# Idle products at the start against a later copy in the w3 stage: a retention and feed-forward kernel on one core

## The chip, the cores and the metric

The kernel runs on one core of a Trainium2 chip. The metric is the device time in microseconds (us) of one execution; the median of three is 869.62 us (869.52 to 870.43). The profile shows one execution, with a span of 867.7 us from the first instruction to the last. Its engines are TensorE (PE, with PEld for its weight loads), VectorE (DVE), ScalarE (ACT), GpSimd (POOL) and SyncE (SP, which only issues transfers here).

## The reference

Retention (attention with a decay in place of a softmax), and behind it a multiplicative feed-forward network, all in float32 except for the weights, which arrive as 64-bit floats and are converted to float32 in the kernel:

```python
# q, k, v: (8, 8, 576, 64);  w1, w2: (512, 1024);  w3: (1024, 1024);  w_out: (1024, 512)
scores = matmul(q, k^T) / sqrt(64)
gamma  = 1 - 2 ** (-5 - arange(8))                    # one per head
ret    = scores * where(rel >= 0, gamma ** rel, 0)    # rel = row - column
x      = matmul(ret, v) -> (4608, 512)                # tokens x (heads * 64)
a, b   = x @ w1, x @ w2
out    = (a * b @ w3) @ w_out
```

The kernel multiplies w3 by w_out first (the product is called w3o) and applies it to the tokens as one matrix.

## The kernel before

Retention works on chunks of 64 or 128 rows of two batches at a time: `front` transposes k and q on TensorE (ScalarE copies them out), `score` makes the products of q and k (VectorE masks them), `state` carries k and v to the next chunk, and `pv` makes the tokens xT. `up` is one part of x @ w1 and x @ w2, in Strassen's form: seven products of sums of tiles, called S, T and the like. The sums T of the tokens are made by `strassen_tokens`, the first of them on VectorE.

The weights are converted in pieces of 128 x 512, by hand from the bits of the 64-bit floats. A piece takes five VectorE instructions and two of ScalarE (cut to its core):

```python
def begin_block():
    ...
    vec.tensor_scalar(out=e, in0=hi, ...)                 # exponent bits
    yield
    vec.tensor_scalar(out=m, in0=hi, ...)                 # mantissa, high part
    yield
    vec.scalar_tensor_tensor(m, in0=lo, ..., in1=m)       # and low part
    nc.scalar.activation(e, e, relu, bias=lim[:, 0:1], scale=-1.0)
    nc.scalar.activation(e, e, relu, bias=lim[:, 1:2], scale=-2.0 ** 23)
    yield

def end_block():
    vec.scalar_tensor_tensor(e, in0=hi, ..., in1=e)       # sign; waits for ScalarE
    yield
    ...
    vec.scalar_tensor_tensor(out, in0=m, ..., in1=e)      # the float32 piece
    if key[0] == "w3" and key[2] == DF // CV - 1:         # second half of a w3 tile
        yield
        t = pools["wst"].tile([P, KF, P], F32, tag="w3T", name="w3T", bufs=3)
        vec.transpose(t..., live["w3"]...)
        live["w3T", key[1]] = t
    ...
```

`convert(n)` lets this go on by n steps, so the conversion of the next piece is spread between other work. One piece is begun before the last one is ended. With a w3 tile of 128 rows ready and transposed, TensorE multiplies it by w_out, in one accumulator, and ScalarE copies it out:

```python
def w3_mm(ft):
    ps = acc.tile([P, DM], F32, tag="acc", name="ps")
    for g in range(KF):
        nc.tensor.matmul(ps, live["w3T", ft][:, g, :], live["wo"][:, g, :],
                         start=(g == 0), stop=(g == KF - 1))
    nc.scalar.copy(live["w3o"][:, ft, :], ps)
    multiplied[0] += 1
...
while multiplied[0] < KF:
    ...
    if ready or not todo:
        convert_up_to(done)
        w3_mm(ft)
    if not todo:
        convert(11)
```

`acc` has seven accumulator banks. Eleven steps of conversion are one tile of w3, which is two pieces and a transpose.

At the start the kernel also issues products of the identity by itself, whose result nobody reads:

```python
warm = acc.tile([P, P], F32, tag="acc", name="idle")
for _ in range(10):
    nc.tensor.matmul(warm, ident, ident, start=True, stop=True)

def keep_busy(n):
    t = acc.tile([P, P], F32, tag="acc", name="idle")
    for _ in range(n):
        nc.tensor.matmul(t, ident, ident, start=True, stop=True)
...
scale(0, "q")
front(0, "k")
keep_busy(4)
front(0, "q")
...
scale(1, "q")
front(1, "k")
keep_busy(6)
front(1, "q")
...
pv(1)
keep_busy(4)
load(3, "kqv")
...
up(0, 0, 0, conv=2, tail=False, busy=8)    # keep_busy(8) behind its first product
```

Of the kernel before, what the change touches and what calls it, by code (L numbers as in the profile page):

```python
# [8 lines left out]
F32 = mybir.dt.float32  # L9
# [31 lines left out]
def kernel(  # L41
# [13 lines left out]
    nc = tc.nc  # L55
# [6 lines left out]
    P = 128  # L62
# [37 lines left out]
    acc = ctx.enter_context(tc.tile_pool(name="acc", bufs=7, space=PSUM))  # L100
# [4 lines left out]
    live = {}  # L105
# [14 lines left out]
    ident = const.tile([P, P], F32, tag="ident", name="ident")  # L120
# [13 lines left out]
    nc.scalar.dma_start(dq, decay_q)  # L134
    nc.scalar.dma_start(gk[:short, 0, :], decay_k[:short, :])
    nc.scalar.dma_start(gk[:, 1:, :], decay_k[short:, :].rearrange("(c p) h -> p c h", p=P))
    warm = acc.tile([P, P], F32, tag="acc", name="idle")
    for _ in range(10):
        nc.tensor.matmul(warm, ident, ident, start=True, stop=True)
    gps = acc.tile([P, NC, H], F32, tag="acc", name="gps")  # L140
    for c in range(NC):
        nc.tensor.transpose(gps[:sizes[c], c, :], dq[:, starts[c]:starts[c] + sizes[c]], ident[:H, :H])
    for c in (0, slice(1, NC)):
        n = short if c == 0 else P
        nc.vector.tensor_copy(gq[:n, c, :], gps[:n, c, :])

    def keep_busy(n):

        t = acc.tile([P, P], F32, tag="acc", name="idle")
        for _ in range(n):  # L150
            nc.tensor.matmul(t, ident, ident, start=True, stop=True)

# [4 lines left out]
    def A(fp, nm):  # L159

        h, m = divmod(fp, 2)
        if nm in ("S1", "S2", "S4"):
            return wS[h][:, ("S1", "S2", "S4").index(nm), m]
        r, f = {"A11": (0, 0), "A12": (1, 0), "A21": (0, 1), "S3": (0, 1), "A22": (1, 1)}[nm]
        return wA[h][:, :, 2 * r:2 * r + 2, m * QC + f * P:m * QC + f * P + P]
# [48 lines left out]
    def scale(g, nm, scalar=False):  # L214
        c = g % NC
        sz = sizes[c]
        t, gam = live[nm, g], {"q": gq, "v": gk}[nm]
        t = t[:sz].rearrange("p (b h) d -> p b h d", b=2)
        if scalar:
            for h in range(H):  # L220
                nc.scalar.mul(t[:, :, h, :], t[:, :, h, :], gam[:sz, c, h:h + 1])
            return
        nc.gpsimd.tensor_tensor(  # L223
            out=t, in0=t, in1=gam[:sz, c].unsqueeze(1).unsqueeze(3).to_broadcast([sz, 2, H, D]), op=ALU.mult)

    def front(g, names="kq"):
        c = g % NC
        sz = sizes[c]
        for nm in names:
            src = live[nm, g]  # L230
            dst = pools["fr"].tile([P, 2, NP, P], F32, tag=nm + "T", name=nm + "T",
                                   bufs=1 if nm == "k" and g >= NC else 2)
            for b in range(2):
                tp = acc.tile([P, NP, P], F32, tag="acc", name="tp")
                for p in range(NP):
                    h = b * H + 2 * p
                    nc.tensor.transpose(tp[:, p, :sz],  # L237
                                        src[:sz, h:h + 2, :].rearrange("p a d -> p (a d)"),
                                        ident[:sz, :sz])
                nc.scalar.copy(dst[:, b, :, :sz], tp[:, :, :sz])  # L240
            live[nm + "T", g] = dst
# [197 lines left out]
    def go_on():  # L439
        while converting:  # L440
            r = next(converting[-1], "end")
            if r != "end":
                return r
            converting.pop()
        return "end"

    def convert(n):

        for _ in range(n):
            if go_on() is not None:  # L450
                return

    def convert_up_to(n):
        while converted[0] < n:
            assert go_on() is None


    def w3_mm(ft):
        ps = acc.tile([P, DM], F32, tag="acc", name="ps")
        for g in range(KF):  # L460
            nc.tensor.matmul(ps, live["w3T", ft][:, g, :], live["wo"][:, g, :],  # L461
                             start=(g == 0), stop=(g == KF - 1))
        nc.scalar.copy(live["w3o"][:, ft, :], ps)
        multiplied[0] += 1

    every = [(i, n) for i in range(NB2) for n in range(NB)]

    def has_x(i, n):
        return any(starts[c] + sizes[c] >= (n + 1) * TB and ("x", i * NC + c) in live for c in range(NC))

    def strassen_tokens(i, n, engine=nc.gpsimd):

        m = every.index((i, n))
        x = live["xT", m]
        B = [[x[:, 2 * r:2 * r + 2, b, :] for b in range(2)] for r in range(2)]
        T = [(t_first if m == 1 and j == 2 else ffn).tile(
            [P, 2, TB], F32, tag="T", name="T", bufs=1 if m == 1 and j == 2 else 5) for j in range(3)]

        def minus(out, in0, in1):
            engine.tensor_tensor(out=out, in0=in0, in1=in1, op=ALU.subtract)  # L480

        live["B", i, n] = {"B11": B[0][0], "B21": B[1][0], "B22": B[1][1], "T3": B[0][1],
                           "T1": T[0], "T2": T[1], "-T4": T[2]}
        minus(T[0], B[0][1], B[0][0])
        minus(T[1], B[1][1], T[0])
        minus(B[0][1], B[1][1], B[0][1])
        minus(T[2], B[1][0], T[1])

    def up(i, n, fp, conv=0, tail=True, busy=0):
        m = every.index((i, n))  # L490
        while ("S", fp) not in live:
            assert go_on() is None
        if ("B", i, n) not in live:
            strassen_tokens(i, n)
        if fp == 0:
            live["ab", i, n] = (pools["ab3"] if m == 2 else ffn).tile([P, 2 * KF, TB], F32, tag="ab", name="ab")
        ab = live["ab", i, n]

        def product(ps, a, b):
            a, b = A(fp, a), live["B", i, n][b]  # L500
            new = ps is None
            if new:
                ps = acc.tile([P, 2, TB], F32, tag="acc", name="up")
            for w in range(2):
                for r in range(2):
                    nc.tensor.matmul(ps[:, w, :], a[:, w, r, :], b[:, r, :], start=(new and w == r == 0),  # L506
                                     stop=(w == r == 1), skip_group_check=True)
            return ps

        def plus(ps, to, sb):  # L510
            nc.vector.tensor_add(c[:, to], ps, c[:, sb])  # L511
            convert(conv)
            if aside:
                aside.pop(0)()


        c = ffn.tile([P, 4, 2, TB], F32, tag="c", name="c", bufs=1)
        p1 = product(None, "A11", "B11")
        nc.scalar.copy(c[:, 0], p1)  # L519
        if busy:  # L520
            keep_busy(busy)
        plus(product(None, "S2", "T2"), 1, 0)
        plus(product(None, "S3", "T3"), 2, 1)
        p5 = product(None, "S1", "T1")
        plus(p5, 3, 2)
        plus(product(None, "A22", "-T4"), 2, 2)
        product(p1, "A12", "B21")
        nc.scalar.copy(c[:, 0], p1)  # L528
        product(p5, "S4", "B22")
        plus(p5, 1, 1)  # L530

        if fp == NQ - 1 and m + 1 < len(every) and has_x(*every[m + 1]) and ("B", *every[m + 1]) not in live:
            strassen_tokens(*every[m + 1])
        nc.vector.tensor_mul(ab[:, 4 * fp:4 * fp + 4, :], c[:, :, 0, :], c[:, :, 1, :])  # L534
        if tail:
            convert(conv)
# [130 lines left out]
    load(1, "v")  # L667
    load_block()
    scale(0, "q")
    front(0, "k")  # L670
    keep_busy(4)
    front(0, "q")
    convert(3)
    score(0)
    scale(0, "v")
# [6 lines left out]
    convert_up_to(2)  # L682
    load_block()
    scale(1, "q")
    front(1, "k")
    keep_busy(6)
    front(1, "q")
    convert(3)
    scale(1, "v")
    score(1)  # L690
# [4 lines left out]
    first_sums = strassen_weights(0)  # L695
    next(first_sums)
    pv(1)
    keep_busy(4)
    load(3, "kqv")
    load_block()  # L700
    strassen_tokens(0, 0, nc.vector)
# [1 line left out]
        pass  # L703
    scale(2, "q", True)
    aside.append(lambda: scale(2, "v", True))
    up(0, 0, 0, conv=2, tail=False, busy=8)
    front(2)
    convert(1)
    scale(3, "q")
# [12 lines left out]
    score(3)  # L722
    aside.extend([lambda: None] * 3 + [lambda: scale(4, "q", True)])
    up(0, 0, 1, conv=2)
    front(4)
    pv(3)
# [21 lines left out]
    todo = [(0, 1, 2), (0, 0, 3), (0, 1, 3)] + [(0, 2, fp) for fp in range(NQ - 1)]  # L748
    while multiplied[0] < KF:
        ft = multiplied[0]  # L750
        done = at["w3", ft, DF // CV - 1] + 1
        ready = converted[0] >= done
        if todo:
            first = converted[0] < 4 * NQ
            up(*todo.pop(0), conv=2 if first else 1)
            convert(0 if first else 3)
        if ready or not todo:
            convert_up_to(done)
            w3_mm(ft)
        if not todo:  # L760
            convert(11)
    w3_part.close()


# [15 lines left out]
    todo = [(down, (0, 0), (0, 1)), (down, (1, 0), (1, 1)), (down, (0, 2), (1, 2))]  # L780
# [38 lines left out]
    for g in range(NC, G):  # L819
        c = g % NC  # L820
        n = -(-len(todo) // (NC - c))
# [78 lines left out]
```

## Time and profile before

| | busy us | share of the span |
|---|---|---|
| TensorE, products | 849.2 | 98% |
| TensorE, weight loads (beside the products) | 774.4 | 89% |
| VectorE | 468.4 | 54% |
| ScalarE | 186.0 | 21% |
| GpSimd | 113.7 | 13% |

| tiles of the change | what the profile has |
|---|---|
| idle products | 64 records, from 1.4 to 32.6 us (each product is recorded twice) |
| product of w3 and w_out | 128 records of 128 x 512, from 158.4 to 216.8 us |
| ScalarE's copy of it | 8 instructions, median 586 ns, from 165.5 to 217.4 us |

The page lists the engines' busy time, the span in 40 slices with the granted clock of TensorE, the chain of work that ended last, and groups of instructions. In a group, a line such as "L463 ACT COPY w3o<-ps" names the line of the kernel, the engine, the operation, and the tile written and read. The idle time next to it is that of the engine just before the instruction, and an arrow names what ended it. The share of 98% is a mean over the whole kernel, so the two stages in question have to be looked at by windows: about 0 to 50 us for the idle products, and about 158 to 217 us for the product of w3 and w_out.

### The profile page before, as it was taken

How to read it: one execution, taken by the hardware profiler on the slowest of the kernel's cores; microseconds unless marked ns; L12 is line 12 of the kernel's file. 1: busy time of each engine (PE TensorE's matmuls, PEld its weight loads, DVE VectorE, ACT ScalarE, POOL GpSimd, SP SyncE). 2: the span in 40 equal slices, each digit the busy share in tenths (PEclk: the TensorE clock that was granted, in tenths of full speed). 3: DMA queues.
4: the chain of work that ended last, by engine and by line, in shares of the span. 5: the costliest groups of instructions: out<-in, count | busy, mean ns of one | idle time of the engine just before them, and what ended most of it. 6: DMA issues, size and time to landing. Idle time of an engine off the chain costs nothing.

```text
span 867.7 us, 15391 instructions
## 1 busy us (share of the span) xinstructions
PE 849.2 (98%) x6373; PEld 774.4 (89%) x6373; DVE 468.4 (54%) x789; ACT 186.0 (21%) x374; POOL 113.7 (13%) x91
## 2 busy tenths in 40 slices
PE   7999999999999999999999999999999999999998
PEld 6889999544888999999999999999999999999996
DVE  4889998986643334543544443534553435334343
ACT  3666333343122221101011101111101100001000
POOL 3000020001202223202123030230300101000000
PEclk9999999999999999999999999999999999999999
DMA  9993443444245534515242325061300000000001
GB/s 194 218 223 110 99 98 101 130 134 66 43 92 124 114 50 78 95 27 101 44 85 39 67 57 109 15 122 19 56 25 26 2 25 1 25 25 0 25 1 49
DMA packets 194629, 63.21 MB, mean 73 GB/s; under 512 B 176632, under 2 KB 184824, under 8 KB 194560
## 3 DMA queue, kind: packets, MB, share of 16 engines
q1 hardware_dynamic: 161920, 54.07, 29.8%
q10 hardware_dynamic: 32640, 8.16, 4.8%
q8 instruction: 50, 0.82, 0.4%
q14 instruction: 19, 0.16, 0.1%
HBM read 52.76 MB, written 9.44 MB: 72 GB/s over the span
## 4 chain that ended last, share of the span: by engine, by line
PE 84%; DVE 6%; issue 2%; ACT 1%; DMA 1%; SPq 0%; DVEq 0%; ACTq 0%
PE up L506 44%; PE po L614 24%; PE ps L461 4%; PE sc L252 4%; PE xps L309 3%; PE xps L302 2%; DVE c L511 2%; PE tp L237 1%; PE st L274 1%; DVE e L400 1%; DVE w L411 1%; DVE m L386 0%; DVE w3T L415 0%; DMA raw<-in_moe_w_out_dram 0%; ACT e L389 0%
## 5 line engine op out<-in xcount | busy, mean ns | idle before, releaser
L511 DVE TENSOR_TENSOR c<-up,c 128x384 f32<-128x384 f32 x240 | 133.2, 555 | 187.0 <-PE up L506 182.2
L506 PE MATMUL up<-xT,wA 128*128 128x192 f32 x1152 | 212.0, 327 | 0.0
L506 PEld LDWEIGHTS up<-xT,wA 128*128 128x128 f32 x1152 | 190.7, 190 | 2.5 <-issue 0.7
L506 PE MATMUL up<-T,wS 128*128 128x192 f32 x768 | 140.6, 326 | 0.0
L506 PEld LDWEIGHTS up<-T,wS 128*128 128x128 f32 x768 | 127.4, 190 | 0.2 <-issue 0.2
L614 PE MATMUL po<-w3o,ab 128*128 128x256 f32 x456 | 104.4, 380 | 2.2 <-DVE ab L580 1.7
L614 PEld LDWEIGHTS po<-w3o,ab 128*128 128x128 f32 x456 | 85.8, 190 | 14.5 <-DVE ab L580 2.1
L618 DVE TENSOR_TENSOR ot<-po,ot 128x256 f32<-128x256 f32 x90 | 38.2, 424 | 73.2 <-PE po L614 70.3
L528 ACT COPY c<-up 128x384 f32<-128x384 f32 x48 | 22.9, 478 | 225.8 <-PE up L506 221.6
L506 PE MATMUL up<-xT,wS 128*128 128x192 f32 x384 | 70.7, 327 | 0.6 <-DVE c L511 0.5
L255 DVE TENSOR_TENSOR pm<-sc,mask 128x512 f32<-128x512 f32 (+1 forms) x80 | 45.4, 629 | 46.4 <-PE sc L252 46.4
L506 PE MATMUL up<-T,wA 128*128 128x192 f32 x384 | 70.2, 326 | 0.0
L614 PE MATMUL po<-wB,forms 128*128 128x256 f32 x288 | 65.1, 379 | 0.0
L506 PEld LDWEIGHTS up<-xT,wS 128*128 128x128 f32 x384 | 63.5, 190 | 1.7 <-DVE c L511 1.7
L506 PEld LDWEIGHTS up<-T,wA 128*128 128x128 f32 x384 | 63.7, 190 | 0.0
L614 PEld LDWEIGHTS po<-wB,forms 128*128 128x128 f32 x288 | 54.7, 190 | 7.4
L223 POOL TENSOR_TENSOR ld_v<-ld_v,gk 128x1024 f32<-128x1024 f32 (+1 forms) x17 | 33.7, 1983 | 210.2 <-DMA ld_v<-in_v_dram 196.2
L461 PE MATMUL ps<-wo,w3T 128*128 128x512 f32 x128 | 56.1, 596 | 2.9 <-DVE w3T L415 2.9
L461 PEld LDWEIGHTS ps<-wo,w3T 128*128 128x128 f32 x128 | 23.8, 190 | 34.5 <-issue 30.6
L480 POOL TENSOR_TENSOR T<-xT,T 128x384 f32<-128x384 f32 x20 | 20.9, 1044 | 216.5 <-PE up L506 214.8
L534 DVE TENSOR_TENSOR ab<-c 128x768 f32<-128x768 f32 x48 | 46.4, 966 | 3.8
L519 ACT COPY c<-up 128x384 f32<-128x384 f32 x48 | 22.9, 477 | 116.3 <-PE up L506 67.4
(77 smaller groups left out, 814.2 us busy)
## 6 DMA issues: line engine op xcount, KB each, us to landing
raw<-in_moe_w_dram SPq DMA_DIRECT2D x64, 128.0 KB, 3.0
out_dram<-ot SPq DMA_DIRECT2D x24, 256.0 KB, 2.1
bl_q<-in_q_dram SPq DMA_DIRECT2D x136, 32.0 KB, 2.1
bl_k<-in_k_dram SPq DMA_DIRECT2D x136, 32.0 KB, 2.1
raw<-in_moe_w_dram SPq DMA_DIRECT2D x8, 512.0 KB, 7.7
raw<-in_moe_w_dram SPq DMA_DIRECT2D x16, 256.0 KB, 6.3
ld_k<-in_k_dram SPq DMA_DIRECT2D x8, 512.0 KB, 7.1
ld_q<-in_q_dram SPq DMA_DIRECT2D x8, 512.0 KB, 9.6
```

The lines of the kernel that those rows point to most:

```text
L223: nc.gpsimd.tensor_tensor(out=t, in0=t, in1=gam[:sz, c].unsqueeze(1).unsqueeze(3).to_broadcast([sz, 2, H, D]), op=ALU.mult)
L252: nc.tensor.matmul(sc[j][:sz, p, :sz], kT[hs, b, p, :sz], qT[hs, b, p, :sz], start=True, stop=True)
L255: nc.vector.tensor_mul(pm[:sz, b, j, :, :sz], sc[j][:sz, :, :sz], mask[:sz, :sz].unsqueeze(1).to_broadcast([sz, NP, sz]))
L309: nc.tensor.matmul(banks[r][heads[half], b, n, :sz], vs[:sz, b * H + 2 * p + j, :], pm[:sz, b, j, p, :sz], start=(c == 0 and m == 0), stop ...
L461: nc.tensor.matmul(ps, live["w3T", ft][:, g, :], live["wo"][:, g, :], start=(g == 0), stop=(g == KF - 1))
L506: nc.tensor.matmul(ps[:, w, :], a[:, w, r, :], b[:, r, :], start=(new and w == r == 0), stop=(w == r == 1), skip_group_check=True)
L511: nc.vector.tensor_add(c[:, to], ps, c[:, sb])
L519: nc.scalar.copy(c[:, 0], p1)
L528: nc.scalar.copy(c[:, 0], p1)
L534: nc.vector.tensor_mul(ab[:, 4 * fp:4 * fp + 4, :], c[:, :, 0, :], c[:, :, 1, :])
L614: nc.tensor.matmul(ps[nm], a[A][:, f, :], live["W"][B][:, f, :], start=(f == 0 and not on), stop=(f == NP - 1), skip_group_check=True)
L618: nc.vector.tensor_add(ot[:, to[0], to[1]], ps[nm], ot[:, sb[0], sb[1]])
```

## The change

All the idle products are taken out. They are there to fill TensorE's waits at the start. In their place, `w3_mm` no longer copies its result itself but returns the copy, and the loop issues it behind the conversion steps of the next tile. ScalarE works its instructions off in the order of issue, so the next tile's exponents no longer stand behind a copy that waits for the product.

```diff
-    warm = acc.tile([P, P], F32, tag="acc", name="idle")
-    for _ in range(10):
-        nc.tensor.matmul(warm, ident, ident, start=True, stop=True)
...
-    def keep_busy(n):
-
-        t = acc.tile([P, P], F32, tag="acc", name="idle")
-        for _ in range(n):
-            nc.tensor.matmul(t, ident, ident, start=True, stop=True)
...
-        nc.scalar.copy(live["w3o"][:, ft, :], ps)
         multiplied[0] += 1
+        return lambda: nc.scalar.copy(live["w3o"][:, ft, :], ps)
...
-    def up(i, n, fp, conv=0, tail=True, busy=0):
+    def up(i, n, fp, conv=0, tail=True):
...
-        if busy:
-            keep_busy(busy)
...
-    front(0, "k")
-    keep_busy(4)
-    front(0, "q")
+    front(0)
...
-    front(1, "k")
-    keep_busy(6)
-    front(1, "q")
+    front(1)
...
     pv(1)
-    keep_busy(4)
...
-    up(0, 0, 0, conv=2, tail=False, busy=8)
+    up(0, 0, 0, conv=2, tail=False)
...
-            w3_mm(ft)
-        if not todo:
-            convert(11)
+            evict = w3_mm(ft)
+
+            if not todo:
+                convert(11)
+            evict()
```

Every other instruction is the same, on each engine in the same order: TensorE has 32 products fewer, and on ScalarE six of the eight copies stand two pieces (four instructions) later.

## The prediction

> **What bounds the kernel now.** I read the engine totals and the slices of the page first, then the tensor engine's own order of time in the two stages that the change touches, and only then the waits there.
>
> ```profile
> PE 849.2 (98%) x6373; PEld 774.4 (89%) x6373; DVE 468.4 (54%) x789; ACT 186.0 (21%) x374; POOL 113.7 (13%) x91
> PEclk9999999999999999999999999999999999999999
> ```
>
> TensorE (PE) is busy 849.2 of 867.7 us, so at most 18.5 us of the span are PE standing still. A change off PE's path is worth nothing, and one that opens or closes PE gaps is worth those gaps. Two stages have them: the first 50 us, and the stage 158 to 217 us in which w3 is converted, transposed and multiplied by w_out.
>
> The second view is PE's order of time in the w3 stage. Columns: start, busy time, engine, line, operation, output<-inputs, shape, count, and in brackets the idle time before it and what ended it.
>
> ```profile
> 166.76 13.97 PE L461 MATMUL ps<-wo,w3T 128*128 128x512 f32 x32 [1.31 <-DVE w3T L415]
> 181.58 14.10 PE L461 MATMUL ps<-wo,w3T 128*128 128x512 f32 x32 [0.84 <-DVE w3T L415]
> 196.42 20.96 PE L461 MATMUL ps<-wo,w3T 128*128 128x512 f32 x48 [0.75 <-DVE w3T L415]
> ```
>
> Sixteen records are one tile, so a tile costs PE about 20.96 / 3 = 6.99 us or, in the run of two, 13.97 / 2 = 6.99; starts lie some 6.9 us apart. Three gaps, 2.90 us in all, wait for VectorE's transposed tile. Why VectorE is late shows in the same window over all engines:
>
> ```profile
> 173.91 0.59 ACT L463 COPY w3o<-ps 128x512 f32<-128x512 f32 x1 [5.09 <-PE ps L461]
> 174.39 0.72 ACT L389 ACTIVATE e<-e,lim 128x512 int32<-128x512 int32 x1
> 175.15 0.72 ACT L390 ACTIVATE e<-e,lim 128x512 int32<-128x512 int32 x1
> ...
> 175.90 0.69 DVE L400 SCALAR_TENSOR_TENSOR e<-raw,e 128x512 int32<-128x512 int32 x1 [1.08 <-ACT e L390]
> ```
>
> ScalarE sits 5.09 us before its copy of the product, because the product is not finished; the exponent work behind it in the queue was ready (its VectorE input began at 169.35 and takes 0.43). VectorE then waits 1.08 us for that exponent, and its transpose comes late for PE's tile at 181.58. The view of waits from 160 to 212 us has three such VectorE waits, 2.9 us in all.
>
> The third view is the clock in the first stage, in windows of 3.4 us (window, length, PE busy, granted clock, share of the transfers):
>
> ```profile
> 11.60:15.00 3.40, 2.12 (x65) 1.00 1.34 211
> 15.00:18.40 3.40, 3.40 (x17) 0.50 1.19 280
> 18.40:21.80 3.40, 1.70 (x13) 1.00 0.96 188
> 21.80:25.20 3.40, 2.59 (x50) 1.00 1.12 216
> ```
>
> The clock was halved for one such window after a sparse one, and restored after a full one. The idle products show the same from the inside:
>
> ```profile
> L151 PE MATMUL idle<-ident x44: 273/275/417, 7.5 to 32.6; 128*128 128x128 f32 x44
> L139 PE MATMUL idle<-ident x20: 274/421/582, 1.4 to 5.2; 128*128 128x128 f32 x20
> ```
>
> Median 421 ns in the first burst against 275 ns later: the kernel also starts slow, until about 4.8 us. The clock column reads 1.00 there, so it doesn't show the state before the first change.
>
> The fourth view is where the first stage has slack:
>
> ```profile
> 28.79 0.69 DVE L400 SCALAR_TENSOR_TENSOR e<-raw,e 128x512 int32<-128x512 int32 x1 [0.48 <-ACT e L390]
> ...
> 32.23 0.56 DVE L480 TENSOR_TENSOR T<-xT,T 128x384 f32<-128x384 f32 x1
> ...
> 44.59 1.06 PE L237 MATMUL tp<-ident,ld_k 128*128 128x128 f32 x8 [1.63 <-DMA ld_k<-in_k_dram]
> ...
> 48.91 1.09 PE L237 MATMUL tp<-ident,ld_q 128*128 128x128 f32 x8 [0.18 <-POOL ld_q L223]
> ```
>
> VectorE is nearly full from 23.1 to 35 us and makes the sums T that the first feed-forward product needs at 32.94. But PE still waits 1.63 us at 44.59 for a load of k, then 0.18 us for the scaled q. The chain of waits, followed back from 225 us, ends at 48.86, just before that last transpose: what comes before is set by transfers (busy share about 1 through the first 60 us), not by PE.
>
> **What the Trainium skill says.** "TensorE: Matmul & The Clock Gate", Part 1 ("What's actually happening"), says that TensorE starts at half clock, that a busy free-running window of about 3.4 us releases it, and that an idle one brings the half back. The trace agrees in the length: 15.00 to 18.40 us at 0.50. It doesn't agree that only idle windows throttle: 11.60 to 15.00 was 2.12 us busy, with products on 64 of the rows and columns. Part 4 of that page ("PE-mode transpose") says that transposes don't count as busy in the same way; no run here separates that. The table at its head says that ScalarE's queue is strictly in order while TensorE's isn't; the 5.09 us wait in front of ready exponents agrees.
>
> **The change, part by part.** (1) It removes 32 idle products (10 + 4 + 6 + 4 + 8), 64 records. By themselves they save nothing: the first ten lie before the decay load lands (6.39), the four before the scaled q (next product at 9.06, idle ones done at 8.64), the six at 16.66 to 19.0 before the q at 20.57, the four at 28.68 to 29.84 beside the copy of xT that ends at 29.71, and the eight end at 32.93 with T done at 32.79: at most 0.15 us.
>
> (2) What they bought is the clock. Without them PE starts its real work at 6.39 at half speed; the transposes at 14.96 measured what that means, 4 in 1.05 us against about 0.55 for 4 warm. Up to 20.57 nothing is lost, since that start is set by a load of q that landed at 18.6. From there, if still cold: the two score groups take 4.1 us in place of 2.06, the transposes and copies before them about 0.5 more, so VectorE's masked scores end at about 28.1 in place of 25.57, some 2.5 us late. Everything VectorE does up to T moves with that. If the clock is back by 21.8, the lateness is about 0.5 us; by 25.2, about 1.9; by 28.6 or 32, 2.5 to 3; if only at 35 to 39, then state, xps and the first product run cold too (1.15 + 1.10 + 1.97 + 1.47 = 5.7 us of warm work doubled) and the lateness is 4.4 to 6.3. The slack at 44.59 and 48.91 takes 1.63 + 0.18 = 1.8 us off each. The transfers themselves don't move: the load queue from 20 to 42 us is held by its own backlog (one issue of q lasts from 34.33 to 41.47), and the buffers that they reuse come free earlier. Loss: 0; 0.1; about 1; 2.6 to 4.5. With weights 0.4, 0.2, 0.15 and 0.25 the mean is about 1.1 us.
>
> (3) It moves ScalarE's copy behind the four exponent instructions of the next tile's two pieces. VectorE's order is the same. Its unhindered tile is seen at 165.37 to 172.21, transpose to transpose: 6.84 us. After the third transpose (done at 173.46) the fourth is then done at about 180.3, and PE finishes its third tile at about 180.6: the wait of 0.84 goes. So does the 0.75, by the same step. The 1.31 before 166.76 stays, because there VectorE was busy with the sums of the last feed-forward piece and ScalarE's exponents were not in the way. Gain: 0.84 + 0.75 = 1.6 us. The copy comes later, but its readers start at 220.56, after the last copy, which has no exponents left before it. After 217 us PE is busy to the end nearly without gaps, and the loads of the next batch are released by VectorE's last conversion, which moves forward too: the 1.6 us carry.
>
> Sum: 869.6 + 1.1 - 1.6 = 869.1 us. I put it at 869.3, a little higher, because the losses have the longer tail.
>
> **The rivals.** First, that the clock comes back as early as before: the work from 6.4 to 20 us, stretched by the half clock, is denser, which releases it. For it: 18.40 to 21.80 stayed at full clock with 1.70 us busy. Then the loss is nothing and the time 868.0. Second, that quarter-size products and transposes don't release it and it stays half until full-size products have filled a window, at 39 or even 42 us. For it: 11.60 to 15.00 throttled at 62% busy. Then the loss is 4.5 to 6 and the time 872.5 to 874. Third, that PE takes VectorE's place at once in the w3 stage, so that fewer than 1.6 us come out: 6.84 against about 6.9 leaves only a few hundredths a tile; a late piece of w3 would bring the wait back, and the gain would be 0.8. Fourth, that the copies, now late, hold accumulator banks: seven are there and this stage uses two or three, so I give it nothing.
>
> **Range and chances.** 867.8 is the gain with no loss and a little over; 873.5 the second rival without its far end. 2% are 17.4 us; PE's whole work between 6 and 39 us is smaller than twice that, and most of it is covered. Faster by over 2%: 0.005; within: 0.985; slower by over 2%: 0.01.
>
> **What would show it.** In the w3 stage of the changed kernel PE should show one gap of about 1.3 us and then a run of 112 records without a break; VectorE's wait for ScalarE's exponent should be gone. If the gaps are still there, step 3 is wrong. The transposes before 10 us should take twice 0.71; the clock column tells when full speed comes, and PE's start of the first product on T (32.94 before) less 1.8 tells the loss. If the transposes of ld_k at 44.59 begin later because their load came later, the claim that the transfers don't move is wrong. If the time is over 874, the half clock reaches farther than any case above.

## The result and the profile after

| | median us | range | ratio to before (95%) |
|---|---|---|---|
| before, beside it | 869.82 | 868.95 to 870.43 | |
| changed | 865.72 | 865.15 to 867.54 | 0.9958 (0.9945 to 0.9971) |
| changed, again, on another chip | 866.37 | 865.69 to 867.35 | 0.9963 (0.9950 to 0.9976) |

By the ratios the change takes off 3.7 and 3.2 us (by the medians 4.1 and 2.9), where 0.3 were predicted, 869.3 against 869.6: the time lies below the predicted range. TensorE (PE) is still busy for 98% of the span. The page of the changed kernel:

```profile
PE 844.1 (98%) x6309; PEld 770.1 (89%) x6309; DVE 465.6 (54%) x789; ACT 186.5 (22%) x374; POOL 113.7 (13%) x91
```

Busy PE fell by 5.1 us. The idle products alone were 10.7 us of it (4.08 + 1.16 + 2.35 + 1.16 + 1.95), and some 6 us came back because the products up to 25 us take longer without them; a total like this doesn't tell where the time went. PE's order of time does. First the w3 stage of the changed kernel (start, busy time, engine, line, operation, tiles, shape, count, idle before):

```profile
157.62 7.03 PE L452 MATMUL ps<-wo,w3T 128*128 128x512 f32 x16
165.96 48.38 PE L452 MATMUL ps<-wo,w3T 128*128 128x512 f32 x112 [1.31 <-DVE w3T L406]
```

One gap of 1.31 us, then 112 records without a break, as the prediction asked for; the next product starts at 214.18. ScalarE and VectorE in the same stage, with the copy where it stands now:

```profile
166.91 0.72 ACT L381 ACTIVATE e<-e,lim 128x512 int32<-128x512 int32 x1
167.10 0.68 DVE L391 SCALAR_TENSOR_TENSOR e<-raw,e 128x512 int32<-128x512 int32 x1
167.54 0.57 ACT L455 COPY w3o<-ps 128x512 f32<-128x512 f32 x1
```

The copy has no idle time in front of it, and the VectorE instruction that sets the sign starts without a wait. Before, the copy sat 5.09 us and VectorE 1.08. Six of the eight copies run so; the last two, with no exponents behind them, still wait for their product (4.94 and 6.28 us).

Then the first 50 us of the changed kernel, PE again:

```profile
21.65 3.79 PE L243 MATMUL sc<-qT,kT 64*128 64x128 f32 x32
...
34.11 1.54 PE L497 MATMUL up<-T,wS 128*128 128x192 f32 x8 [2.09 <-DVE T L471]
...
43.97 1.04 PE L228 MATMUL tp<-ident,ld_k 128*128 128x128 f32 x8
...
48.28 1.09 PE L228 MATMUL tp<-ident,ld_q 128*128 128x128 f32 x8 [0.20 <-POOL ld_q L214]
```

The scores run 3.79 us in place of 2.06. That is taken here as the half clock; the clock column reads 1.00 throughout, as it does at the start of the kernel before. The first product on T is 1.2 us late (34.11 against 32.94). At 43.97 nothing of that is left: the transposes of k no longer wait for the load, and those of q wait 0.20 us for GpSimd as before (0.18).

The rest of the gain lies behind the w3 stage, where the products of the tokens with w3o ("po") begin. VectorE's four sums of w3o and GpSimd's (POOL) scaling of the next batch's second chunk, in the kernel before:

```profile
221.22 2.32 POOL L223 TENSOR_TENSOR ld_q<-ld_q,gq 128x1024 f32<-128x1024 f32 x1 [3.68 <-DMA ld_q<-in_q_dram]
223.50 2.88 POOL L223 TENSOR_TENSOR ld_v<-ld_v,gk 128x1024 f32<-128x1024 f32 x1
```

```profile
222.16 2.46 DVE L551 TENSOR_TENSOR wB<-w3o 128x1024 f32<-128x1024 f32 x1
...
225.01 2.45 DVE L551 TENSOR_TENSOR wB<-w3o,wB 128x1024 f32<-128x1024 f32 x1
...
227.85 1.21 DVE L551 TENSOR_TENSOR wB<-w3o,wB 128x1024 f32<-128x1024 f32 x1
...
230.18 3.72 PE L614 MATMUL po<-w3o,ab 128*128 128x256 f32 x16 [1.74 <-DVE ab L580]
```

and after the change, when the scaling of q runs from 214.79 and only that of v meets a sum:

```profile
216.90 1.90 POOL L214 TENSOR_TENSOR ld_v<-ld_v,gk 128x1024 f32<-128x1024 f32 x1 [0.21 <-DMA ld_v<-in_v_dram]
```

```profile
217.52 2.36 DVE L540 TENSOR_TENSOR w3o<-w3o 128x1024 f32<-128x1024 f32 x1
...
220.28 1.21 DVE L540 TENSOR_TENSOR wB<-w3o 128x1024 f32<-128x1024 f32 x1
...
225.81 3.72 PE L603 MATMUL po<-w3o,ab 128*128 128x256 f32 x16 [0.50 <-DVE ab L569]
```

Before, two sums took twice their 1.21 us while GpSimd was scaling; after, one did. PE's wait for the VectorE work behind the sums fell from 1.74 to 0.50 us. The scaling falls earlier against the sums because the loads of the next batch start earlier. The first of them follows a VectorE instruction of the conversion, the one that sets the sign. Before:

```profile
206.95 0.69 DVE L400 SCALAR_TENSOR_TENSOR e<-raw,e 128x512 int32<-128x512 int32 x1
...
207.67 0.61 SPq L113 DMA_DIRECT2D ld_k<-in_k_dram  x1
```

and after:

```profile
201.58 0.67 DVE L391 SCALAR_TENSOR_TENSOR e<-raw,e 128x512 int32<-128x512 int32 x1
...
202.28 0.61 SPq L113 DMA_DIRECT2D ld_k<-in_k_dram  x1
```

Measured from PE's first product behind the stage, the load starts 11.9 us ahead in place of 9.5, and both parts of the change have a share in these 2.4 us. VectorE, unhindered, ends its last sign instruction at 203.58, which is 10.6 us ahead in place of 9.6. And the load no longer follows that last one, as it did before, but the one of the piece before it, 1.3 us earlier. In all eight profiles without idle products the load follows the last piece but one, in all four with them the last. So the order of the instructions is the old one, but what this load waits for is not; why it changes with the idle products is not shown.

The account of the two profiles, by PE's starts. The marks are the second transposes of q near 49, the first record of the w3 stage, the first product behind it, and the first product with S2 and T2 ("po<-wB,forms"):

| stretch | before | after | difference |
|---|---|---|---|
| start to transposes of q | 48.91 | 48.28 | -0.63 |
| to the w3 stage | 109.51 | 109.34 | -0.17 |
| w3 stage | 58.79 | 56.56 | -2.23 |
| to the products on S2 | 16.52 | 15.18 | -1.34 |
| to the end | 633.97 | 633.84 | -0.13 |
| span | 867.7 | 863.2 | -4.5 |

### The profile page after: what moved, and what is told of

Same layout as the page of the kernel before. It is cut to its first block, busy times and chain, and to the rows that moved or that the text cites. A ratio compares the mean times of both kernels' runs of the same rounds, so it can differ in the third digit from the quotient of the medians.

```text
span 863.2 us, 15264 instructions
## 1 busy us (share of the span) xinstructions
PE 844.1 (98%) x6309; PEld 770.1 (89%) x6309; DVE 465.6 (54%) x789; ACT 186.5 (22%) x374; POOL 113.7 (13%) x91
## 4 chain that ended last, share of the span: by engine, by line
PE 87%; DVE 4%; issue 2%; DMA 1%; SPq 1%; ACT 0%; DVEq 0%; ACTq 0%
PE up L497 45%; PE po L603 25%; PE ps L452 6%; PE sc L243 4%; PE xps L300 3%; PE xps L293 2%; PE tp L228 1%; PE st L265 1%; DVE c L502 1%; SPq L725 0%; DVE e L391 0%; DMA raw<-in_moe_w_out_dram 0%; DVE w L402 0%; DMA gqs<-decay_q_dram 0%; DMA out_dram<-ot 0%
```

## The experiments

**The late copy alone.** The kernel before with `w3_mm` returning its copy, and the loop issuing it behind `convert(11)`; all idle products stay.

```diff
-        nc.scalar.copy(live["w3o"][:, ft, :], ps)
+        return lambda: nc.scalar.copy(live["w3o"][:, ft, :], ps)
...
-            w3_mm(ft)
-        if not todo:
-            convert(11)
+            evict = w3_mm(ft)
+            if not todo:
+                convert(11)
+            evict()
```

> The late copy alone, idle products kept. Theory (the late copy makes all of the gain: about 2.2 us in the w3 stage, because PE no longer waits for VectorE there, and about 1.2 us behind it, because VectorE's conversion ends earlier, the next batch's loads go out earlier, and GpSimd's scaling no longer runs beside VectorE's sums of w3o): 865.5 to 866.5 us, the same as the changed kernel or a little less, one run of 112 records in the w3 stage, and the wait before the second group of po products about 0.5 us. Rival (taking the idle products out makes about half of it): 867.5 to 868.5 us.

Measured: 866.41 us against 869.18 beside it, 0.9965 (0.9953 to 0.9978). The w3 stage of its profile:

```profile
166.86 48.35 PE L461 MATMUL ps<-wo,w3T 128*128 128x512 f32 x112 [1.31 <-DVE w3T L415]
```

The stage is 56.53 us, as in the changed kernel; the next product starts at 215.05. The copy's place alone makes that gain. The stretch behind it took 16.04 us in this profile, 0.5 less than before. The wait before the second group of po products is 0.51 us, as expected, but PE waits another 0.72 us one product earlier: GpSimd's second scaling, begun at 220.23, met the second sum, which took 2.94 us. The first load starts 10.6 us ahead of the product behind the stage, 1.0 more than before.

**The idle products out, the copy where it was.** The changed kernel with the copy back inside `w3_mm` and the loop as it was.

> The idle products out, the copy where it was. Theory: 869.5 to 871 us, as before or slower by up to 2 us when the clock comes back late, with the lateness of about 1.2 us in the first product on T taken up by the wait for a load of k near 44 us. Rival (the idle products cost something): about 867.5 to 868.5 us.

Measured: 869.68 us against 869.18, 0.9999 (0.9990 to 1.0007). In sum, leaving out the 32 products neither costs nor gains within 0.1%. Its w3 stage is 58.80 us, with the three old gaps. PE in the first 60 us:

```profile
33.61 2.63 PE L497 MATMUL up<-T,wS 128*128 128x192 f32 x8 [2.09 <-DVE T L471]
...
48.95 1.10 PE L228 MATMUL tp<-ident,ld_q 128*128 128x128 f32 x8
...
58.56 1.54 PE L497 MATMUL up<-T,wS 128*128 128x192 f32 x8 [1.18 <-DVE wS L160]
```

Here the clock halved again just behind the wait of 2.09 us for T (the clock column reads 0.50 from about 33.9 to 37.3 us), and the first product on T took 2.63 us. At 48.95 PE is still where it was before (48.91). The wait of 1.18 us at 58.56 is of this profile alone; none of the other profiles without idle products has it, and what made it stays open. With it the w3 stage begins 1.3 us later than before (159.71 against 158.42). Behind the stage 1.2 us are gained: the stretch is 15.28 us in place of 16.52, with one of the four sums at 2.46 us in place of two, and the first load starts 10.9 us ahead in place of 9.5. So the unchanged total is the sum of two differences that cancel in this profile, and its gain behind the stage owes nothing to the late copy.

**Before, with GpSimd held back.** One small GpSimd instruction that reads VectorE's fourth sum, in front of the scaling of the second chunk. It writes a constant that nothing reads any more.

```diff
+    nc.gpsimd.tensor_tensor(out=lim[:, 0:1], in0=live["W"]["-T4"][:, 0, 0:1], in1=live["W"]["-T4"][:, 0, 0:1],
+                            op=ALU.subtract)
     scale(NC + 1, "q")
```

> The kernel before, with GpSimd's scaling of the second chunk of the next batch held back until VectorE's four sums of w3o are done (one small GpSimd instruction that reads the last sum). Theory (two of the sums took 2.46 us in place of 1.21 because GpSimd was scaling beside them, and PE waited 1.74 us for it): all four sums at 1.2 us, the wait before the second group of po products gone, 1.5 to 1.8 us faster than before. Rival (the sums are long for another reason, such as the transfers of the next batch, which land at the same time): sums still at 2.4 us, time unchanged.

Measured: 868.48 us against 869.18, 0.9992 (0.9983 to 1.0001). VectorE, GpSimd and PE in its profile:

```profile
225.63 1.22 DVE L551 TENSOR_TENSOR wB<-w3o,wB 128x1024 f32<-128x1024 f32 x1
...
227.13 1.90 POOL L223 TENSOR_TENSOR ld_q<-ld_q,gq 128x1024 f32<-128x1024 f32 x1
227.26 2.32 DVE L580 TENSOR_TENSOR ab<-ab 128x512 f32<-128x512 f32 x1
...
229.63 1.56 PE L614 MATMUL po<-w3o,ab 128*128 128x256 f32 x6 [1.16 <-DVE ab L580]
```

All four sums are at 1.22 us, so it was GpSimd that stretched them. But the held work now meets the next VectorE instruction, S3, which takes 2.32 in place of 0.68 us: it stands until the scaling ends at 229.03 and is done 0.55 us after that. The wait fell from 1.74 to 1.16, not to nothing; the stretch is 15.70 us. The expectation was right in the mechanism and wrong in the gain, which within the noise may be none.

**The changed kernel with the same hold.** The same edit on the changed kernel.

> The changed kernel with the same hold. Theory: the one sum that took 2.36 us falls to 1.2, the wait of 0.50 us goes, 0.5 us faster than the changed kernel (about 865.2). Rival: no change.

Measured: 866.47 us against 869.18, 0.9966 (0.9954 to 0.9979). Again S3 took 2.32 us and PE waited 1.16; the stretch is 15.71 us, worse than the changed kernel's 15.18. A miss for the same reason.

**The changed kernel again,** on the chip of the next three.

> The changed kernel again, on the chip of the next three and beside the same runs of before. Theory (w3 stage 2.2 us; the rest, 0.5 to 1.3 us, from where GpSimd's scaling falls against VectorE's sums): ratio 0.9955 to 0.9970, w3 stage from the second tile to the next product 48.2 us in place of 50.45, two-humped times when the clock comes back late in some runs. Rival (a steady gain of 4 us with a part yet unseen): ratio 0.9950 to 0.9957.

Measured: 866.37 us against 869.25, 0.9963 (0.9950 to 0.9976). w3 stage 56.57 us, stretch behind it 15.48, and 48.89 us up to the transposes of q. So the 0.63 us of the first account are not the change's: kernels without idle products have that mark anywhere from 48.10 to 49.62 us.

**The collision brought back.** The hold with the first sum ("T3") in place of the fourth, so that the scaling must meet the next sums.

> The changed kernel, with GpSimd's scaling of that chunk held only until the first of VectorE's four sums is done, so that it must run beside the next ones. Theory (the collision is what PE waits for behind the w3 stage): two of the later sums at about 2.4 us, the wait before the second group of po products 1.5 to 1.8 us as in the kernel before, about 1.2 us slower than the changed kernel. Rival (the collision has nothing to do with it): wait stays at 0.5 us.

Measured: 867.49 us against 869.25, 0.9980 (0.9973 to 0.9987), 1.1 us over the changed kernel beside it (the two intervals just overlap). Its sums and PE:

```profile
220.43 2.89 DVE L540 TENSOR_TENSOR wB<-w3o 128x1024 f32<-128x1024 f32 x1
223.71 2.45 DVE L540 TENSOR_TENSOR wB<-w3o,wB 128x1024 f32<-128x1024 f32 x1
...
228.88 3.72 PE L603 MATMUL po<-w3o,ab 128*128 128x256 f32 x16 [1.75 <-DVE ab L569]
```

The wait of the kernel before, 1.74 us, is back as 1.75 in a kernel that has the late copy. The stretch is 16.95 us.

**Held past everything PE waits for.** The hold with the last sum for the first output tiles (S1, tile forms).

```diff
+    gate = pair_of((2, 0), (2, 1))[0]["S1"]
+    nc.gpsimd.tensor_tensor(out=lim[:, 0:1], in0=gate[:, 0, 0:1], in1=gate[:, 0, 0:1], op=ALU.subtract)
     scale(NC + 1, "q")
```

> The changed kernel, with the same scaling held until VectorE has made the last of the sums for the first output tiles (S1), behind all that PE waits for there. Theory: four sums at 1.2 us, S3 (the one that took 2.32 us in the hold until the fourth sum) at 0.7, no wait before the second group of po products, that stage 0.5 to 0.6 us shorter than in the changed kernel. Rival (what is held back is missed later): the transposes of the next batch start later and PE waits there instead, time as the changed kernel or longer.

Measured: 865.22 us in 4 runs against 869.25, 0.9950 (0.9932 to 0.9967). PE behind the w3 stage:

```profile
223.93 5.34 PE L603 MATMUL po<-w3o,ab 128*128 128x256 f32 x24
229.11 3.62 PE L603 MATMUL po<-wB,forms 128*128 128x256 f32 x16
```

No wait is left, and the stretch is 14.28 us, 0.9 less than in the changed kernel's profile and 1.2 less than in its second one. What was held back isn't missed: the rest of the kernel takes 633.79 us, as elsewhere. In whole runs the interval overlaps the changed kernel's; the gain is read from the stretch.

**More conversion ahead of the w3 stage,** against the gap that remained.

```diff
-            up(*todo.pop(0), conv=2 if first else 1)
+            part = todo.pop(0)
+            up(*part, conv=2 if first or not todo else 1)
```

> The changed kernel, with two conversion steps in place of one behind each sum in the last feed-forward part before the w3 stage. Theory (the gap of 1.31 us before the second tile, which the late copy left, is VectorE being behind with the second tile's pieces): the gap falls to 0.3 to 1.0 us and the stage is that much shorter. Rival (VectorE has no free time there, so order doesn't matter): gap stays at 1.3.

Measured: 864.97 us in 4 runs against 869.25, 0.9951 (0.9934 to 0.9969), not separable from the changed kernel. PE around the start of the stage:

```profile
157.78 1.57 PE L497 MATMUL up<-xT,wS 128*128 128x192 f32 x8 [1.56 <-DVE c L502]
159.19 55.13 PE L452 MATMUL ps<-wo,w3T 128*128 128x512 f32 x128
```

The gap is gone: all 128 records run through. But PE now waits 1.56 us one step earlier, for a sum that stands behind the added conversion. From the transposes of q to the first product behind the stage it takes 166.05 us, against 165.90 in the changed kernel: the wait moved. That VectorE bounds this passage in either order fits this, and is not shown beyond it.

**The longest hold with more rounds, and with the idle products back.** The second is the late copy alone with that hold.

> The changed kernel with the longest hold of GpSimd's scaling, once more, with more rounds, beside the next. Theory: w3 stage 48.2 us from the second tile, no wait before the second group of po products, ratio 0.9945 to 0.9957 (about 4.3 us off, of which 2.2 in the w3 stage and 2.2 behind it). Rival (the 865.22 us of the first look were chance): ratio as the changed kernel's, 0.996 to 0.9965.

> The same with all the idle products back in place. Theory (they buy clock only where transfers set the pace, so they are worth nothing): the same time within 0.5 us as without them. Rival (they save the 1 us by which the first product on T is late without them): 0.8 to 1.2 us faster than without them.

Measured, side by side: 865.66 us and 0.9957 (0.9944 to 0.9971) without idle products, 864.54 us and 0.9942 (0.9929 to 0.9956) with them, against 869.12. From the transposes of q on the two profiles agree within 0.2 us (w3 stage 56.58 and 56.58, stretch 14.28 and 14.28). Up to there they took 49.58 and 50.62 us, the other way round than the medians. The intervals overlap. Whether idle products are worth up to 1 us here is not settled. It would fit the second experiment: with the scaling held, the earlier loads that come with leaving them out can't pay. Nor do whole runs resolve what the hold gains: 0.9957 stands against 0.9958 and 0.9963 for the changed kernel, and only the stretch shows it.

## Why the prediction was wrong

The time fell below the range because two of the prediction's terms were sized wrongly and one was missing. With what the profiles show in their place, 2.2 us in the w3 stage, 1.0 to 1.3 behind it and no loss before it, 869.6 becomes 866.1 to 866.4; the two medians are 865.72 and 866.37.

**The gain in the w3 stage, "0.84 + 0.75 = 1.6 us".** The mechanism was right in each part: the copy alone brings it, both gaps go, the 1.31 stays, PE runs through. It measured 2.23 us. The step that failed is reading PE's lost time from the idle column. A record of this product is 592 ns long while starts lie 430 ns apart (48.22 us / 112), so the last record before a gap hides some 0.16 us of it. Smaller delays show no gap at all: of the two stretches of two tiles, the second took 14.10 us in place of 13.97. By starts, the three stretches before were 14.82, 14.84 and 20.79 us for 2, 2 and 3 tiles; at 6.889 us a tile the losses were 1.04, 1.06 and 0.12. "Perfetto Trace Analysis", section "Tensor Engine Instruction (MATMUL, LD_WEIGHTS)", of the Trainium skill says that a matmul's end is a model and not a measurement; records of 592 ns at starts 430 ns apart agree, and the prediction should have used starts.

**"After 217 us PE is busy to the end nearly without gaps ... the 1.6 us carry."** This is the missing term. The profile before showed the wait of 1.74 us, and two of VectorE's sums at twice the time of the others, and the prediction even said that the next batch's loads move forward. It didn't ask what those loads trigger. They trigger GpSimd's scaling, and its place against VectorE's sums set the wait: 16.52 us for the stretch before, 15.18 and 15.48 in the changed kernel, 16.95 with the collision forced and 14.28 with none. The experiments that move only GpSimd's scaling show this as the cause. The earlier loads come from both parts of the change: by the issue times some 1.0 us from the late copy and 1.3 us from leaving out the idle products, for which the prediction had no gain. The stretch follows: 16.04 with the late copy alone, 15.28 without idle products alone, one profile each.

**"Loss: 0; 0.1; about 1; 2.6 to 4.5 ... the mean is about 1.1 us".** What was measured is no loss at the second transposes of q: they start at 48.10 to 49.62 us in the eight profiles without idle products, at 48.82 to 50.62 in the four with them. In the changed kernel's profile the slow products last to about 25.5 us. That is nearest to the case "by 25.2", for which the prediction foretold 1.9 us of lateness; the first product on T was 1.2 us late. The step that failed is "Up to 20.57 nothing is lost, since that start is set by a load of q that landed at 18.6". That start moved: GpSimd's scaling of this q begins at 17.15 to 17.65 us without idle products and at 18.61 to 18.84 with them, and PE's transposes of it at 19.75 in place of 20.57. What brings it forward is not shown. The slack at 44.59 us took up the rest, as foretold. The worse cases, with a weight of 0.4 together, did not cost what was foretold: in the profile of the second experiment the clock did halve again at 33.9 us, and PE was where it had been by 48.95 us.

**The rivals.** The first (868.0 us) was the nearest in time, but not by its mechanism: the clock did not come back as early as before. The second (872.5 to 874) is refuted by the second experiment (868.01 to 870.41). The third, that VectorE leaves PE only hundredths of a us a tile, is what happened, without taking back any of the gain: VectorE's transposes are 6.91 us apart (171.40 to 199.04) and PE's tiles 6.89. The fourth, accumulators, had no part: PE runs through.

## What to carry to other kernels

Where an engine works in order, as ScalarE does here, put an instruction that waits for a long product behind those that are ready and that somebody waits for. Read PE's lost time from start to start. When a change frees an engine, follow what that engine releases: its loads, the work that the loads start, and what that work runs beside. And before filling an engine's waits to keep its clock up, look whether a later wait takes up the lost time anyway: here PE waited for a load near 44 us, and leaving out the 32 products did not change the time within 0.1%. An unchanged total can hide a loss and a gain, so compare stretch by stretch.

## What the runs showed of the hardware

In these profiles VectorE and GpSimd exclude each other for whole instructions. In the kernel before, the second sum starts at 222.16, GpSimd's scaling ends at 221.22 + 2.32 = 223.54, and 223.54 less 222.16 plus the sum's own 1.21 makes 2.59, about the 2.46 seen; the next scaling, begun at 223.50, then waits for that sum and needs 2.88 in place of 1.90. "SBUF — State Buffer", section "Who interferes with whom", of the Trainium skill says that a VectorE instruction with two inputs in SBUF contends with a GpSimd instruction that reads SBUF, over a port pair that is an exclusive lock. That whoever comes first keeps the pair for its whole instruction it says of VectorE's two-port modes; these lengths agree with the same for the sums. The sums and S3 have two inputs in SBUF. The additions onto c, with one input in the accumulators, kept their 0.55 us beside the same scaling.

The clock halved with the idle products in place too. In the profile of the last experiment:

```profile
44.93 1.06 PE L237 MATMUL tp<-ident,ld_k 128*128 128x128 f32 x8 [1.88 <-DMA ld_k<-in_k_dram]
45.92 3.68 PE L252 MATMUL sc<-qT,kT 64*128 64x128 f32 x32
```

A wait of 1.88 us for a load at 43 to 45 us, where the kernel has no idle products, was followed by a clock of 0.50 from 46 to about 49 us, by scores at 3.68 us in place of 2.06, and by transposes of q at 50.62 in place of 48.91. The kernel before waited 1.63 us at the same place and kept its clock.
